# Last weight rows transferred once, rows fetched four slots ahead, routing's product at another slot

## The chip, the cores and the metric

The kernel runs on one core of a Trainium2 chip. The metric is the device time of one execution in microseconds; a lower number is better. The core's engines are TensorE (matmuls; PE in the profile, PEld its weight loads), VectorE (DVE), ScalarE (ACT), GpSimd (POOL) and SyncE (SP), which here only issues transfers. Sixteen DMA engines carry the transfers.

## The reference

Three layers follow one another. The first is a gated linear attention (an mLSTM) over 4 batches, 8 heads, 768 steps, head size 40:

```
m_new = max(f + m, i);  f_s = exp(f + m - m_new);  i_s = exp(i - m_new)
C = f_s * C + i_s * (v k^T);   n = f_s * n + i_s * k
y = sigmoid(o) * (C q) / max(|n q|, 1)
```

The second is a dense layer over 3072 tokens: `h = x @ w_in` (320 to 2048), `x2 = (h * sigmoid(h)) @ w_out` (2048 to 320). The third is a mixture of 8 experts, where each token goes to one expert only:

```
logits = x2 @ w_gate;  e = argmax(logits);  g = softmax(logits)[e]
out = g * (relu(x2 @ w1[e]) @ w2[e])        # w1[e]: 320 x 1024, w2[e]: 1024 x 320
```

Everything is float32.

## The kernel before

Matmuls run in float16 on numbers that are split into a high and a low half; the products of the halves are summed in PSUM. The 320 rows of a weight matrix are two blocks of 128 rows and a last block of 64. For the last 64 rows, the high half lies on partitions 0 to 63 and the low half on partitions 64 to 127 of the same block, so that one matmul takes both.

**The loop.** Steps are cut into 6 chunks of 128 for each of the 4 batches; a chunk and a batch make an attention unit (`n = 4c + b`). The dense layer makes a pass over chunk c with 16 blocks `f` of the inner dimension. Each block has two slots of a plan (`p`), so that a pass has 32 slots. In the even slot TensorE runs `l1` (8 matmuls, L959, tile ps_h), what `run_at(p)` finds planned, and then `l2` of the block two earlier (12 matmuls into ps_y, L1000 to L1005); in the odd slot it runs what is planned there. A function that returns another one has that one run in the next slot (`late`). The order on TensorE, ScalarE, VectorE and SP is that of the program, written out by hand.

The steps of an attention unit are planned at its base `p`: scores S at p and p + 1 (L294, read by VectorE at L296), I at p + 2 (L304, read at L308), C at p + 3 (L353, read at L367), PV at p + 5 (L318, read at L324), X at p + 12 (L394, read by ScalarE at L397 and VectorE at L400). Except for the first units, the bases are 8 slots apart, so that within a chunk's pass S stands at slots 7 and 8, I at 9, C at 10, X of the unit before at 11, PV at 12, S of the next unit at 15. All of them take their PSUM tile from `ps_at`, which has two buffers, in turn. A tile can be written when the readers of the one two tiles earlier are through.

**Routing.** `rows(c)` (L844) is planned into the pass of chunk c + 1 in eight steps, two slots apart, from slot 5 on: `experts`, `scale`, `weights`, `place`, and four `halves`. `place` (L874) runs two small matmuls (L877, L878; the routing's product) into a ps_at tile and four VectorE operations that give each token the number of its row in the tensor rows_x. `halves` splits a batch's 128 results and scatters them to rows_x (L929). For the last chunk these steps are called by hand in the next stage.

**The experts.** The tokens of an expert stand in rows_x in groups of 128 (slots of the list `line`, 28 in all). For three slots (EARLY) the rows are known before the last chunk's routing; `fetch_early` (L1021) loads them, planned at slot 23 of the last pass. For each other slot `fetch` (L1184) reads a row number into a register of SP, loads the 128 rows transposed (L1189) and their scales (L1194). Rows go to buffers in turn (`xT_b`, L1182): four tiles that the attention used (Ks[1], Qs[0], Qs[1], Ks[0]). A slot has two halves of 32 matmuls (`m_half`, L1209) and 24 matmuls of the second layer (`m_l2`, L1228 to L1230). In the loop at L1329, turn i fetches slot i + 3 first.

**The experts' weights.** `load_w` (L532) loads a quarter of an expert: 256 rows of w1, the last 64 rows of w1 (L541, L546), and 256 rows of w2, into a staging buffer. `go` converts it on ScalarE (L552, L553), and `tail` makes the low halves on VectorE (L556, L560, L564). The last 64 rows are loaded twice, to partitions 0 to 63 and 64 to 127, by a source whose outermost dimension has two copies. Sixteen quarters are loaded during the loop and 32 in the expert stage, where `low_and_load`, `split` and `load` keep up to six in flight; one is converted in each turn, two in the odd ones.

Of the kernel before, what the change touches and what calls it, by code (L numbers as in the profile page):

```python
# [8 lines left out]
F32 = mybir.dt.float32  # L9
F16 = mybir.dt.float16  # L10
BF16 = mybir.dt.bfloat16
I32 = mybir.dt.int32
AF = mybir.ActivationFunctionType
# [10 lines left out]
SW1, SW2 = 2.0**10, 2.0**12  # L24
# [3 lines left out]
def bcast0(ap, n):  # L28

    return bass.AP(tensor=ap.tensor, offset=ap.offset, ap=[[0, n]] + list(ap.ap))  # L30
# [3 lines left out]
def mlstm_moe_kernel(ctx, tc, q, k, v, ig, fg, og, w_in, w_out, w_gate, w1, w2, out):  # L34
    nc = tc.nc
# [3 lines left out]
    NC = S // CH  # L39
    DM = H * D  # L40
    FF = w_in.shape[1]
    NF = FF // 128
# [7 lines left out]
    GF = F2 // NG  # L50
# [3 lines left out]
    NE = len(EARLY)  # L54
# [7 lines left out]
    const = ctx.enter_context(tc.tile_pool(name="const", bufs=1))  # L62
# [25 lines left out]
    START, ATTN, FIRST = 0, 2, 4  # L88
# [3 lines left out]
    def carve(where, shape, dtype=F32):  # L92

        n = 1
        for d in shape:
            n *= d
        size = 2 if dtype is F16 else 4
        a = carved[where]
        carved[where] += n * size
        assert carved[where] <= limit[where], (where, carved[where])  # L100
        x = w_all if dtype is F16 else F32V if dtype is F32 else w_all.bitcast(dtype)
        x = x[:, a // size:a // size + n]
        return x if len(shape) == 1 else x.rearrange("p (a b) -> p a b", a=shape[0])

    def turns(views):

        i = 0
        while True:
            yield views[i % len(views)]
            i += 1  # L110
# [7 lines left out]
    for e in range(E):  # L118
# [12 lines left out]
        out=tri, in_=ones, pattern=[[1, 128]], compare_op=ALU.is_gt, fill=0.0, base=0, channel_multiplier=-1  # L131
# [5 lines left out]
    Qs = [const.tile([128, H, 128], F16, name=f"Qs{i}") for i in range(2)]  # L137
    Ks = [const.tile([128, H, 128], F16, name=f"Ks{i}") for i in range(2)]
# [10 lines left out]
    wol = carve(FIRST, (NF, NO), F16)  # L149
    xt_b = turns([carve(FIRST, (6, 512), F16) for _ in range(2)])  # L150
    vw_b, hb_b = carve(FIRST, (H, D1)), carve(FIRST, (H, D1))
    y_b = turns([carve(FIRST, (384,)), const.tile([128, 384], F32, name="y2")])
    cl_b = carve(FIRST, (H, D1), F16)[0:D]
    vh_b, vl_b = [turns([carve(FIRST, (H, D1), F16) for _ in range(3)]) for _ in range(2)]
    late_at = carved[FIRST] // 4
# [376 lines left out]
    def load_w(k, g, e, ts=None):  # L532

        cs = slice(g * GF, (g + 1) * GF)
        if ts is None:
            ts = stg.tile([128, WI], F32, tag="wi", name="e12")
        t = ts[:, 0:3 * GF].rearrange("p (j f) -> p j f", j=3)
        t2 = ts[:, 3 * GF:3 * GF + 2 * DM].rearrange("p (j d) -> p j d", j=2)
        if isinstance(e, int):
            nc.sync.dma_start(out=t[:, 0:2, :], in_=w1[e, 0:256, cs].rearrange("(j p) f -> p j f", p=128))  # L540
            nc.sync.dma_start(out=t[:, 2, :], in_=bcast0(w1[e, 256:320, cs], 2))  # L541
            nc.sync.dma_start(out=t2, in_=w2[e, cs, :].rearrange("(j p) d -> p j d", p=128))
        else:
            ee = bass.ds(e, 1)
            nc.sync.dma_start(out=t[:, 0:2, :], in_=w1[ee, 0:256, cs].rearrange("e (j p) f -> p (e j) f", p=128))
            nc.sync.dma_start(out=t[:, 2, :], in_=w1[ee, 256:320, cs].to_broadcast([2, 64, GF]))  # L546
            nc.sync.dma_start(out=t2, in_=w2[ee, cs, :].rearrange("e (j p) d -> p (e j) d", p=128))
        o1 = w1c[k][:, :, cs]
        o2 = w2c[k][:, 2 * g:2 * g + 2]

        def go():
            nc.scalar.activation(out=o1[:, 0:3, :], in_=t, func=AF.Copy, scale=SW1)  # L552
            nc.scalar.activation(out=o2[:, :, 0, :], in_=t2, func=AF.Copy, scale=SW2)  # L553

            def tail():
                nc.vector.scalar_tensor_tensor(  # L556
                    out=o1[:, 3:5, :], in0=t[:, 0:2, :], scalar=SW1, in1=o1[:, 0:2, :],
                    op0=ALU.mult, op1=ALU.subtract,
                )
                nc.vector.scalar_tensor_tensor(  # L560
                    out=o1[64:128, 2, :], in0=t[64:128, 2, :], scalar=SW1, in1=o1[64:128, 2, :],
                    op0=ALU.mult, op1=ALU.subtract,
                )
                nc.vector.scalar_tensor_tensor(  # L564
                    out=o2[:, :, 1, :], in0=t2, scalar=SW2, in1=o2[:, :, 0, :], op0=ALU.mult, op1=ALU.subtract
                )
            return tail
        return go

    import contextlib  # L570
    with contextlib.nullcontext():

        wg_t = const.tile([128, 3, E], F32, name="wg_t")
        with tc.tile_pool(name="gate", bufs=1) as gp:
# [25 lines left out]
            for i in range(3):  # L600
# [4 lines left out]
                out=mneg, in_=mneg, pattern=[[0, 4], [1, CH]], compare_op=ALU.is_ge, fill=-1e30,  # L605
# [74 lines left out]
            def first(b, g):  # L680
# [95 lines left out]
                out=E_t[:, 1:, :], in0=E_t[:, 1:, :], scalar1=1.0 / (SQ * SQ), scalar2=None, op0=ALU.mult  # L776
# [12 lines left out]
        def at(p, fn, *args):  # L789
            plan.setdefault(p, []).append((fn, args))  # L790
# [6 lines left out]
        for n in range(B, NC * B):  # L797
            cb = divmod(n, B)
            p = base[n]
# [23 lines left out]
        for f in range(NF):  # L823
# [7 lines left out]
            p = 2 * f - 2  # L831
# [4 lines left out]
        for i in range(4 * NG):  # L836
            p = 2 * NF * 2 + 10 * i if i < 2 * NG else 2 * NF * (NC - 1) - 7 + 7 * (i - 2 * NG) // 2
# [100 lines left out]
            return [experts, scale, weights, place] + [lambda b=b: halves(b) for b in range(nb)]  # L938

        for c in range(NC - 1):  # L940
            for i, fn in enumerate(rows(c)):
                at(2 * NF * (c + 1) + 5 + 2 * i, fn)
        at(2 * NF * (NC - 1) + 23, lambda: fetch_early())

        gt = {}
        l2b = {}
# [74 lines left out]
        def fetch_early():  # L1021
            for i, (e, n) in enumerate(EARLY):
                o = e * ER + 128 * (n + 1)
                r = rows_x[o:o + 128, :]
                xT[e, n] = (Qs + Ks)[i][:, 0:6, :]
                nc.sync.dma_start_transpose(out=xT[e, n], in_=r.bitcast(F16)[:, 0:768])
                xm[e, n] = xms[:, i, :]
                nc.sync.dma_start(out=xm[e, n], in_=r[:, 384:386])
            pe = ps_at.tile([128, E], F32, tag="at", name="ps_e")
            nc.tensor.matmul(pe, ones, cum[:, NTT - B, :], start=True, stop=True)  # L1030
            nc.vector.memset(done, 0.0)
            for e, n in EARLY:
                nc.vector.tensor_scalar(
                    out=done[:, e:e + 1], in0=pe[:, e:e + 1], scalar1=128.0 * (n + 1), scalar2=None, op0=ALU.min
                )
# [22 lines left out]
        p = 0  # L1058
# [3 lines left out]
        for c, b0, b1 in passes:  # L1062
# [17 lines left out]
            if c == 0:  # L1080
                for r in rowt:
# [4 lines left out]
                    out=rows_x.rearrange("(e r) w -> r e w", e=E)[0:128],  # L1086
                    in_=rowt[0].unsqueeze(1).to_broadcast([128, E, RW]),
# [4 lines left out]
        while plan or late:  # L1092
            p = min([*plan, *late])
# [85 lines left out]


        hT, place_of = {}, {}
        xT_b = turns([x[:, 0:6, :] for x in Ks[1:] + Qs + Ks[:1]])  # L1182

        def fetch(i, row):  # L1184

# [96 lines left out]
        def low_and_load():  # L1282

            if w_low:
                t, place = w_low.pop(0)
                t()
                load(place)

        def get(i):
            if NE <= i < len(line):  # L1290
                fetch(line[i][0], line[i][2])

        def second(i):
            m_l2(line[i][0], line[i][1], line[i][3])
# [3 lines left out]
        with tc.manual_schedule(engines=by_hand):  # L1298

            for cf in todo:  # L1300
                l2(*cf)
            for i in range(2):
                rowt.append(th_v[i][:, 0:RW])
                nc.gpsimd.memset(rowt[-1][:, 352:384], 0.0)
            experts, scale, weights, place, *halves = rows(NC - 1)
            half = lambda i, r: m_half(line[i][0], line[i][1], r)
            t = half(0, 0)
            experts()
            t()
            t = half(0, 1)  # L1310
            place()
            scale()
            weights()
            t()
            h = [x() for x in halves[0:2]]
            t = half(1, 0)
            h.pop(0)()
            t()
            h += [x() for x in halves[2:]]
            h.pop(0)()  # L1320
            t = half(1, 1)
            h.pop(0)()
            h.pop(0)()
            count()
            t()
            second(0)
            get(NE)
            get(NE + 1)
            for i in range(2, len(line)):  # L1329
                get(i + 3)  # L1330
                t = half(i, 0)
                low_and_load()
                t()
                if i > 5 and i % 2:
                    split()
                t = half(i, 1)
                t()
                if i > 5 and i % 2:
                    low_and_load()
                if i == 3:  # L1340
                    later_slots()
                split()
                if more and i > 4:
                    load(more.pop(0))
                second(i - 1)
            second(len(line) - 1)
        n_slots = nc.values_load(eni[0:1, E - 1:E], min_val=0, max_val=128 * NSLOT)
        with tc.If(n_slots > 128 * ND):
            for i in range(ND, NSLOT):
                name, k, row, no = later(i)  # L1350
                e = nc.sync.value_load(evi[0:1, i:i + 1], min_val=0, max_val=E - 1)
# [36 lines left out]
```

## Time and profile before

| | us |
|---|---|
| median of 3 runs | 732.72 (732.57 to 733.4) |
| the profiled execution | 736.41 |
| its span, first to last instruction | 734.7 |
| TensorE busy in the span | 671.2 (91%) |
| VectorE busy | 529.7 (72%) |
| ScalarE busy | 372.7 (51%) |
| DMA queue of SP and ScalarE (q1), share of 16 engines | 63.8% |

Times of rows count from the start of the span. Busy time says how long an engine worked; an engine's idle time matters only where the next work on the path waits. The clock of a stretch (PEclk) is the granted share of TensorE's full 2.4 GHz, so 0.5 is 1.2 GHz. The DMA share is the mean over sixteen engines; a transfer's whole time counts in the stretch in which its packets start, so a short stretch can have more than 1.

### The profile page before, as it was taken

The page shows a single profiled execution, that of the slowest core. Times are in us where ns is not written, and L with a number is a line of the kernel's source. Part 1 is how long each engine was busy: PE and PEld are TensorE (multiplying, and loading weights), DVE is VectorE, ACT ScalarE, POOL GpSimd, SP SyncE. Part 2 cuts the span into 40 slices and gives each one's busy share as a digit, 9 for nine tenths or more (in the row PEclk, how much of TensorE's full clock was granted, in tenths as well). Part 3 has the DMA queues.
Part 4 walks back from the last instruction along what each step waited for, and adds up shares of the span by engine and source line. Part 5 has one row for each costly group of instructions (what it writes and reads, how often), then busy time and mean ns, then how long its engine had stood idle before and what let it go on. Part 6 is the DMA issues. An engine that isn't in the chain of part 4 may idle for free.

```text
span 734.7 us, 15579 instructions
## 1 busy us (share of the span) xinstructions
PE 671.2 (91%) x5840; PEld 480.0 (65%) x5840; DVE 529.7 (72%) x1262; ACT 372.7 (51%) x816; POOL 100.6 (14%) x134
## 2 busy tenths in 40 slices
PE   3868899999899989998999999999999898998993
PEld 2734666776476655665666665556888786877882
DVE  7775779987888787799887975975677655665631
ACT  4644365655575655675676635564334333533410
POOL 3100011100121002110210110020311111111111
PEclk9758599999999988999999999999999999999998
DMA  8768979884565655976587520544279799999900
GB/s 158 128 150 205 201 144 212 196 198 88 106 139 127 138 100 106 166 149 131 116 180 162 133 80 14 128 146 105 80 145 194 166 189 171 186 170 190 160 24 15
DMA packets 242828, 102.82 MB, mean 140 GB/s; under 512 B 181141, under 2 KB 236632, under 8 KB 242744
## 3 DMA queue, kind: packets, MB, share of 16 engines
q1 hardware_dynamic: 239380, 92.98, 63.8%
q0 software_dynamic: 2880, 8.68, 3.5%
q8 instruction: 48, 0.79, 0.5%
q14 instruction: 36, 0.29, 0.2%
q10 hardware_dynamic: 484, 0.08, 0.1%
HBM read 71.64 MB, written 11.59 MB: 113 GB/s over the span
## 4 chain that ended last, share of the span: by engine, by line
PE 70%; DVE 13%; DMA 8%; ACT 3%; SPq 3%; issue 2%; POOL 0%; POOLq 0%; DVEq 0%; ACTq 0%
PE ps_h L959 19%; PE ps_m L1209 12%; PE ps_y L1003 5%; PE ps_y L1005 5%; PE ps_y L1004 5%; PE ps_pv L318 5%; DMA Ks<-rows_x 3%; PE ps_y L1000 3%; PE ps_m L1228 3%; PE ps_m L1230 3%; PE ps_m L1229 3%; DMA Qs<-rows_x 2%; PE ps_wg L517 1%; DMA wi<-in_moe_w_in_dram 1%; DMA w_all<-lam_d 1%
## 5 line engine op out<-in xcount | busy, mean ns | idle before, releaser
L959 PE MATMUL ps_h<-w_all 128*128 128x512 f16 x768 | 193.1, 392 | 8.2 <-ACT w_all L466 5.1
L959 PEld LDWEIGHTS <-w_all 128*128 128x128 f16 x768 | 73.5, 100 | 85.1 <-issue 10.6
L1209 PEld LDWEIGHTS <-w_all 128*128 128x128 f16 x1792 | 106.8, 101 | 19.1 <-DMA Ks<-rows_x 9.9
L1005 PE MATMUL ps_y<-w_all 128*128 128x328 f16 x332 | 101.1, 305 | 0.3 <-DVE w_all L986 0.3
L1004 PE MATMUL ps_y<-w_all 128*128 128x328 f16 x332 | 101.1, 305 | 0.0
L1003 PE MATMUL ps_y<-w_all 128*128 128x328 f16 x332 | 100.9, 305 | 0.0
L1214 ACT ACTIVATE hh<-ps_m 128x512 f16<-128x512 f32 x56 | 33.3, 596 | 126.5 <-PE ps_m L1209 114.9
L975 ACT ACTIVATE w_all<-ps_h 128x512 f32<-128x512 f32 x83 | 49.2, 592 | 67.0 <-PE ps_h L959 66.8
L978 DVE SCALAR_TENSOR_TENSOR w_all<-w_all,ps_h 128x512 f32<-128x512 f32 x83 | 56.7, 683 | 29.3 <-ACT w_all L975 28.0
L1215 DVE SCALAR_TENSOR_TENSOR hl<-ps_m,hh 128x512 f16<-128x512 f32 x56 | 38.6, 690 | 48.5 <-ACT hh L1214 48.1
L983 ACT ACTIVATE w_all<-w_all 128x512 f16<-128x512 f32 x83 | 51.6, 622 | 30.7 <-DVE w_all L978 28.9
L1229 PE MATMUL ps_m<-w_all,hh 128*128 128x320 f16 x224 | 67.0, 299 | 0.0
L1230 PE MATMUL ps_m<-w_all,hl 128*128 128x320 f16 x224 | 67.0, 299 | 0.0
L1228 PE MATMUL ps_m<-w_all,hh 128*128 128x320 f16 x224 | 67.0, 299 | 0.0
L1209 PE MATMUL ps_m<-Ks,w_all 128*128 128x128 f16 x896 | 55.9, 226 | 8.9 <-DMA Ks<-rows_x 6.9
L986 DVE SCALAR_TENSOR_TENSOR w_all<-w_all 128x512 f16<-128x512 f32 x83 | 57.9, 697 | 5.6 <-ACT w_all L983 5.3
L1209 PE MATMUL ps_m<-Qs,w_all 128*128 128x128 f16 x896 | 54.1, 222 | 6.0 <-DMA Qs<-rows_x 4.2
L1240 POOL DMA_INDIRECT out_dram<-ym,sid x28 | 32.0, 1142 | 169.5 <-DVE sid L1239 153.7
L318 PEld LDWEIGHTS ps_pv<-w_all 128*128 128x128 f32 x384 | 51.2, 210 | 4.3 <-issue 1.7
L318 PE MATMUL ps_pv<-w_all 128*128 128x41 f32 x384 | 51.2, 296 | 0.4 <-DVE w_all L296 0.4
L241 ACT ACTIVATE w_all<-w_all,bias_t 128x128 f32<-128x128 f32 x160 | 50.2, 391 | 2.4 <-POOL w_all L207 2.3
L207 POOL TENSOR_SCALAR_AFFINE_SELECT w_all<-w_all 128x1024 f32<-128x1024 f32 x20 | 22.8, 1142 | 183.1 <-DMA w_all<-lam_d 130.0
(219 smaller groups left out, 1159.6 us busy)
## 6 DMA issues: line engine op xcount, KB each, us to landing
e<-in_moe_w_dram SPq DMA_DIRECT2D x35, 320.0 KB
w_all<-lam_d SPq DMA_DIRECT2D x20, 512.0 KB
e<-in_moe_w_dram SPq DMA_DIRECT2D x35, 256.0 KB
w_all<-in_moe_w_out_dram SPq DMA_DIRECT2D x16, 320.0 KB
e<-in_moe_w_dram SPq DMA_DIRECT2D x35, 128.0 KB
w_all<-in_moe_w_dram SPq DMA_DIRECT2D x13, 320.0 KB
wi<-in_moe_w_in_dram SPq DMA_DIRECT2D x8, 512.0 KB
w_all<-in_k_dram SPq DMA_DIRECT2D x24, 160.0 KB
```

The lines of the kernel that those rows point to most:

```text
L318: nc.tensor.matmul(pv[:, h, :], u["lam"][:, h, :], u["v"][:, h, :], start=True, stop=True)
L959: nc.tensor.matmul(ps, a, x, start=(i == 0), stop=(i == len(terms) - 1))
L978: nc.vector.scalar_tensor_tensor(out=th, in0=th, scalar=1.0, in1=ps, op0=ALU.add, op1=ALU.mult)
L983: nc.scalar.activation(out=gh, in_=th, func=AF.Copy, scale=SG)
L986: nc.vector.scalar_tensor_tensor(out=gl, in0=th, scalar=SG, in1=gh, op0=ALU.mult, op1=ALU.subtract)
L1003: nc.tensor.matmul(ps, gh[:, ts], woh[:, f, :], start=(f == 0), stop=False)
L1004: nc.tensor.matmul(ps, gh[:, ts], wol[:, f, :], start=False, stop=False)
L1005: nc.tensor.matmul(ps, gl[:, ts], woh[:, f, :], start=False, stop=(f == NF - 1))
L1209: nc.tensor.matmul(ps[:, jj, :], w1c[k][:, a, f * 128:f * 128 + 128], x[:, m, :], start=(n == 0), stop=(n == len(terms) - 1),)
L1228: nc.tensor.matmul(ps, hh[:, f, :], w[:, 0, :], start=(f == 0), stop=False)
L1229: nc.tensor.matmul(ps, hh[:, f, :], w[:, 1, :], start=False, stop=False)
L1230: nc.tensor.matmul(ps, hl[:, f, :], w[:, 0, :], start=False, stop=(f == NF2 - 1))
```

## The change

Three edits. First, the last 64 rows of w1 are loaded once, to partitions 0 to 63. ScalarE's conversion becomes two instructions, of 128x512 and of 64x256, and VectorE makes the low half by reading partitions 0 to 63 and writing 64 to 127. Second, a fifth buffer for fetched rows, the tile y2, which the attention used before, and fetches four slots ahead instead of three: three fetches stand before the loop instead of two. Third, the eight steps of `rows(c)` stand at slots 5, 7, 9, 13, 14, 16, 18, 20 instead of 5, 7, 9, 11, 13, 15, 17, 19, and `fetch_early` at 24 instead of 23.

```
-    y_b = turns([carve(FIRST, (384,)), const.tile([128, 384], F32, name="y2")])
+    y2 = const.tile([128, 384], F32, name="y2")
+    y_b = turns([carve(FIRST, (384,)), y2])
...
-            nc.sync.dma_start(out=t[:, 2, :], in_=bcast0(w1[e, 256:320, cs], 2))
+            nc.sync.dma_start(out=t[0:64, 2, :], in_=w1[e, 256:320, cs])
...
-            nc.sync.dma_start(out=t[:, 2, :], in_=w1[ee, 256:320, cs].to_broadcast([2, 64, GF]))
+            nc.sync.dma_start(out=t[0:64, 2, :], in_=w1[ee, 256:320, cs].rearrange("e p f -> p (e f)"))
...
-            nc.scalar.activation(out=o1[:, 0:3, :], in_=t, func=AF.Copy, scale=SW1)
+            nc.scalar.activation(out=o1[:, 0:2, :], in_=t[:, 0:2, :], func=AF.Copy, scale=SW1)
+            nc.scalar.activation(out=o1[0:64, 2, :], in_=t[0:64, 2, :], func=AF.Copy, scale=SW1)
...
-                    out=o1[64:128, 2, :], in0=t[64:128, 2, :], scalar=SW1, in1=o1[64:128, 2, :],
+                    out=o1[64:128, 2, :], in0=t[0:64, 2, :], scalar=SW1, in1=o1[0:64, 2, :],
...
-            for i, fn in enumerate(rows(c)):
-                at(2 * NF * (c + 1) + 5 + 2 * i, fn)
-        at(2 * NF * (NC - 1) + 23, lambda: fetch_early())
+            for i, fn in zip((5, 7, 9, 13, 14, 16, 18, 20), rows(c)):
+                at(2 * NF * (c + 1) + i, fn)
+        at(2 * NF * (NC - 1) + 24, lambda: fetch_early())
...
-        xT_b = turns([x[:, 0:6, :] for x in Ks[1:] + Qs + Ks[:1]])
+        xT_b = turns(
+            [Ks[1][:, 0:6, :], y2.bitcast(F16).rearrange("p (j t) -> p j t", j=6)]
+            + [x[:, 0:6, :] for x in Qs + Ks[:1]]
+        )
...
             get(NE + 1)
+            get(NE + 2)
             for i in range(2, len(line)):
-                get(i + 3)
+                get(i + 4)
```

## Rows read from the trace of the kernel before

**Rows 1.** The page: the chain that ended last, and a group of TensorE's matmuls.
```profile
PE 70%; DVE 13%; DMA 8%; ACT 3%; SPq 3%; issue 2%; POOL 0%; POOLq 0%; DVEq 0%; ACTq 0%
...
L959 PE MATMUL ps_h<-w_all 128*128 128x512 f16 x768 | 193.1, 392 | 8.2 <-ACT w_all L466 5.1
```

**Rows 2.** Waits of TensorE: who for whom, us in total, times, longest.
```profile
PE ps_m L1209 <- DMA Ks<-rows_x: 6.9, 3, 3.5
...
PE ps_r L877 <- DVE w_all L367: 2.9, 2, 1.5
...
PE ps_r L877 <- DVE w_all L296: 2.7, 1, 2.7
```

**Rows 3.** Windows, expert stage: us, busy us of PE PEld DVE ACT POOL, PEclk, DMA, GB/s.
```profile
509.40:723.20 213.80, 198.40 (x2468) 170.29 (x2466) 126.55 (x280) 78.83 (x127) 35.11 (x31) 0.98 0.79 145
...
512.00:518.00 6.00, 4.05 (x69) 3.68 (x67) 5.34 (x28) 3.01 (x7) 0.00 (x0) 1.00 0.00 0
...
542.00:544.00 2.00, 1.61 (x14) 1.06 (x12) 1.97 (x4) 0.25 (x1) 0.80 (x1) 1.00 0.74 147
...
584.00:592.00 8.00, 5.37 (x56) 4.85 (x55) 2.52 (x6) 0.68 (x2) 1.18 (x1) 0.79 0.84 150
618.00:626.00 8.00, 4.49 (x51) 4.42 (x51) 2.85 (x6) 1.00 (x2) 1.18 (x1) 0.79 1.11 190
666.00:674.00 8.00, 4.92 (x57) 4.62 (x55) 3.02 (x6) 1.19 (x2) 1.18 (x1) 0.79 0.85 148
```

**Rows 4.** Windows, for the last two columns (DMA share, GB/s).
```profile
552.00:554.00 2.00, 2.00 (x40) 2.00 (x38) 1.59 (x4) 0.60 (x1) 1.01 (x1) 1.00 1.04 314
...
597.20:678.40 81.20, 71.79 (x875) 61.65 (x873) 47.02 (x84) 31.97 (x50) 11.77 (x10) 0.96 1.04 178
632.00:634.00 2.00, 2.00 (x36) 1.92 (x33) 1.48 (x2) 0.77 (x2) 0.33 (x1) 1.00 0.14 48
...
695.00:700.00 5.00, 5.00 (x59) 4.09 (x57) 1.99 (x6) 1.97 (x4) 0.00 (x0) 1.00 0.62 130
```

**Rows 5.** Timeline of TensorE: first-layer matmuls of two slots (start, us, what).
```profile
550.74 3.74 PE L1209 MATMUL ps_m<-Ks,w_all 128*128 128x128 f16 x64
...
557.57 3.74 PE L1209 MATMUL ps_m<-Ks,w_all 128*128 128x128 f16 x64
```

**Rows 6.** Timeline of SP: issues of fetches and loads (start, us, what).
```profile
493.89 1.24 SPq L1026 DMA_TRANSPOSE Qs<-rows_x  x1
...
597.21 1.53 SPq L1189 DMA_TRANSPOSE Qs<-rows_x  x1
...
669.51 1.27 SPq L1189 DMA_TRANSPOSE Ks<-rows_x  x1
...
672.26 0.38 SPq L545 DMA_DIRECT2D e<-in_moe_w_dram  x1
...
674.66 0.37 SPq L545 DMA_DIRECT2D w_all<-in_moe_w_dram  x1
...
678.36 2.49 SPq L1189 DMA_TRANSPOSE Ks<-rows_x  x1
```

**Rows 7.** Around the routing's product: three windows, one row of VectorE's timeline.
```profile
192.00:200.00 8.00, 5.17 (x48) 2.41 (x47) 5.91 (x15) 1.23 (x2) 0.00 (x0) 0.79 0.81 143
...
270.00:281.00 11.00, 11.00 (x42) 6.88 (x41) 6.29 (x18) 4.52 (x13) 2.25 (x3) 0.53 0.62 142
...
344.00:348.00 4.00, 2.57 (x19) 1.54 (x17) 3.60 (x11) 1.43 (x4) 0.00 (x0) 1.00 1.03 184
...
347.32 0.54 DVE L400 SCALAR_TENSOR_TENSOR w_all<-ps_x,w_all 128x384 f16<-128x384 f32 x1
```

**Rows 8.** Groups by shape on ScalarE: count | busy us, mean ns.
```profile
L552 ACT ACTIVATE w_all<-e 128x768 f16<-128x768 f32 x35 | 29.2, 835 | 0.7 <-DMA e<-in_moe_w_dram 0.7
...
L466 ACT ACTIVATE w_all<-w_all 64x128 f16<-64x128 f32 x24 | 7.3, 304 | 0.3
...
L466 ACT ACTIVATE w_all<-w_all 128x512 f16<-128x512 f32 x8 | 5.0, 623 | 5.0 <-DVE w_all L428 5.0
```

## The prediction

> **What bounds the kernel now.** I read the page first, then the waits of TensorE, then windows over the last stage, then the DMA shares there, and last the places where the routing's product stands. The page's chain is 70% TensorE and 8% DMA [rows 1]: the kernel is bound by TensorE, so what can be won is the time in which TensorE stands still or runs at its lower clock. The waits show two causes that the change touches: the expert matmuls (L1209) wait for the transposed rows, and the routing's product (L877) waits for VectorE's reads of ps_at buffers, 2.7 us once and 2.9 us in two further rounds [rows 2]. In the expert stage, 213.8 us long, TensorE is busy 198.40 us [rows 3]. Of the 15.4 us idle, 1.95 lie at its start around the last routing (512 to 518) and 0.39 at 542 to 544; the other 13.1 are stalls ahead of a slot's first matmul. After the three longest the granted clock falls from 2.4 to 1.2 GHz for a while: 0.79 on the mean of each of three stretches of 8 us [rows 3], (1 - 0.79) x 8 = 1.7 us each, 5.0 in all. A little of that low clock lies in the idle time itself, so both together make 17.5 us.
>
> Why are the rows late? From 597.2 to 678.4 the DMA share is 1.04 [rows 4], so the fetch waits in a full queue. But the bytes don't explain it: 178 GB/s there against 314 GB/s at share 1.04 between 552 and 554. In between stand stretches like 632 to 634, where the share is 0.14 and the rate 48 GB/s [rows 4]: two engines of sixteen (0.125) still work on something and the rest stand. That fits L541 and L546, whose outermost dimension is two copies: 64 rows of 1 KB on each of two engines. A transposed fetch has its part on every engine, so I read it as landing only when these two are through.
>
> The count confirms it. Two slots bring three loads and two fetches. L541's 131 KB at 48 GB/s are 2.7 us on the two engines; the other 590 KB of a load at 314 GB/s are 1.9 us on every engine; a fetch takes about 1.1 us (695 to 700, mostly three fetches, 0.62 x 5 = 3.1 us) [rows 4]. Sum on the two engines: 3 x 4.6 + 2 x 1.1 = 16.0 us. SP's fetches of every second slot stand at 597.21 and, five pairs later, at 678.36: 16.2 us a pair [rows 6]. TensorE needs 6.83 us a slot without a stall [rows 5], 13.7 a pair. The two engines are 2.5 us a pair too slow, and SP, blocked behind them, falls back until every second slot stalls.
>
> **The change part by part.** *The last 64 rows once.* The transfer halves to 65 KB and its outermost dimension becomes 64 rows. No row shows a 64-row transfer from memory in this queue. If it spreads like the 128-row ones, it is 65 KB at 314 GB/s, 0.2 us; at worst, all on one engine at half of 48 GB/s, it is 2.7 us again. I take 0.2: rows of whole partitions are what the 128-row transfers have, and those run at the full rate. Then a pair costs 3 x (1.9 + 0.2) + 2 x 1.1 = 8.5 us on each engine, well under 13.7, and the stalls have no cause. What is late next is SP's own issuing: a fetch takes it 2.75 us (669.51 to 672.26), a load 2.40 (672.26 to 674.66) [rows 6], 2 x 2.75 + 3 x 2.40 = 12.7 a pair, still under 13.7. So all 17.5 us go.
>
> The Trainium skill, DMA: Bandwidth & Descriptors, section Rules for kernel authors, says that a leading broadcast of c copies confines a transfer to c engines and that an outermost size that is a multiple of 16 uses all; by it the new transfer is 0.2 us, and an estimate by it gives the same 17.5. The same section speaks against the change where it advises 128 partitions and 1 MiB a transfer, and calls transfers under 64 KB mostly overhead; the new one sits on that border. The trace has 14 engines of 16 standing during the old transfer [rows 4], so an overhead would have room, and it would change no term.
>
> *ScalarE and VectorE.* The conversion of 128x768 (0.835 us) becomes 128x512 and 64x256 [rows 8]. 128x512 is 0.623; 64x256 lies between 0.304 (64x128) and 0.623, by elements about 0.41. That is 0.2 us more for each of 48 conversions, 9.5 us of ScalarE (bounds 0.09 and 0.41, 4.4 and 19.7 us). ScalarE is on 3% of the chain [rows 1]; in the expert stage it is busy 78.83 of 213.8 us [rows 3], and its idle time hides it. In the loop, where conversions precede VectorE's work ahead of a wait, a few can show: 0.6 us. If ScalarE had no idle time, all 9.5 would count. VectorE's third operation keeps its size and reads other partitions: 0, with nothing in the rows for a gain or a loss.
>
> *Four ahead in five buffers.* The buffer of slot i+4 is that of slot i-1, as the buffer of i+3 was, so no new wait for a buffer. One fetch more is issued ahead of the first load, 2.75 us of SP, while the loads are needed many slots later. It gives one slot, 6.83 us, of further lead. With the queue relieved it hides nothing that is left: 0. If the queue were not relieved it would be worth up to 6.8 us once.
>
> *The product between two units.* At slot 11 it takes the next ps_at buffer right behind C and X, and waits until VectorE has read C (L367) or, in the first round, the second scores (L296) [rows 2]. At slot 13 it stands behind PV and twelve ps_y matmuls and takes the buffer of X, which VectorE reads at 347.32 for 0.54 us (third round) [rows 7], some 3 us earlier. Behind it on TensorE stand the next ps_h matmuls, which no longer wait. First round: of 2.7 us part returns, since C now needs the buffer that the product waited for; eight ps_h matmuls lie between, 193.1 / 96 = 2.0 us [rows 1], so 0.7 returns and 2.0 go; the low clock around it, 0.79 over 8 us [rows 7], partly idle, gives 1.3: 3.3. Second round: 1.5 of wait, and the low clock that follows, (1 - 0.53) x 11 = 5.2 [rows 7]: 6.7. X's own shorter wait there stays, but the third round had 1.4 of wait at clock 1.00 [rows 7], so a wait of that size need not lower the clock. Third round: 1.4. Fourth and fifth: 0. Sum 11.4. Bounds: 0 if VectorE's backlog stops the next TensorE instruction instead, 12.1 if nothing returns. The row scatters move one slot later and the early fetch too, some 1.7 us; it is issued at 493.89 and used from 509.4 [rows 6, 3], so that costs 0.
>
> **Sum.** -17.5 - 11.4 + 0.6 = -28.3. The profiled execution took 736.41 us (span 734.7 and 1.7 around it): 708.1. The median of the runs is 732.72, 3.7 us less than the profiled one, so some term is smaller in them. If none of these, 704.4; if the long low-clock stretch (5.2) is what they lack, 709.6. I take 706, its own range 700 to 712.
>
> **The rivals.** *VectorE takes the product's place.* In the third round VectorE is busy 3.60 of 4 us [rows 7]; whatever TensorE wins it may wait for at the next read. Then only the expert stage gains: 732.7 - 17.5 = 715.2. Against it: between these spots TensorE is the one that is full.
>
> *The fetches stay late.* The 64 rows don't spread, or SP paces. Then the product's 11.4 and one slot's lead, 6.8, remain: 732.7 - 11.4 + 0.6 - 6.8 = 715.1, or 721.9 if the lead is eaten too. For it: SP's 12.7 is not far below 13.7. Against: SP's spacing of 16.2 is the two engines' sum.
>
> *Slower: the product stalls at its new place.* At slot 13 VectorE has the seven operations of PV's end in its queue, and the product's buffer could come free behind them. If each of four rounds then waits 2.7 us and loses 5.2 to the clock, that is 31.6 against 12.1 now, +19.5, against -17.5: 734.7. It decides from about 4.4 us of further cost a round. Against it: the read that frees the buffer stands ahead of PV's end in VectorE's order.
>
> **How the numbers follow.** Forecast 0.82; VectorE 0.06; late fetches 0.06; slower 0.04; no difference by both halves eaten 0.02. The range 700 to 717 takes in the first two rivals' 715 and leaves out the rest. Faster by over 0.2% (1.5 us, about what can be told from no change) 0.94, within it 0.02, slower 0.04.
>
> **What would show it.** Right: no stretch with a share of 0.14 at 48 GB/s in the expert stage, no L1209 wait on rows_x beyond a microsecond, expert slots 6.83 us apart, the stage about 196 us, no L877 wait between 190 and 350, clock 1.00 at the place of 270 to 281. Wrong: fetches still 16 us a pair; new waits of S or C on VectorE of the size of those gone; a low clock elsewhere.

## The result

The changed kernel takes 707.62 us (median of 4 runs, 699.15 to 714.71) beside 732.64 us of the kernel before: a ratio of 0.962, with a 95% interval of 0.9536 to 0.9704. The forecast was 706. Ratios and their intervals go by the fast runs of a kernel alone, medians by all of its runs, so that where many runs are slow the two can differ. The profiled execution took 707.71 us, 28.7 us less than that of before (736.41); the sum of the prediction was 28.3. The near agreement of these two is partly luck, as the experiments show.

The page of the changed kernel: the chain, the waits of TensorE in the expert stage (from 500 us on), and windows of the loop and of the stage (columns as in [rows 3]).

```profile
PE 79%; DVE 12%; ACT 3%; DMA 2%; issue 2%; SPq 1%; POOL 0%; POOLq 0%; DVEq 0%; ACTq 0%
```

```profile
PE ps_m L1214 <- DVE hl L1220: 1.4, 2, 0.8
PE ps_r L879 <- DVE cum L872: 0.5, 1, 0.5
PE ps_m L1214 <- DMA e<-in_moe_w_dram: 0.4, 1, 0.4
```

```profile
163.20:499.60 336.40, 331.41 (x2494) 212.22 (x2492) 279.22 (x683) 206.62 (x459) 46.54 (x46) 1.00 0.55 124
499.60:694.20 194.60, 192.24 (x2469) 165.89 (x2466) 124.58 (x280) 81.29 (x159) 35.11 (x31) 1.00 0.62 149
...
270.00:281.00 11.00, 11.00 (x95) 6.60 (x93) 10.07 (x30) 7.86 (x19) 2.91 (x3) 1.00 0.48 110
584.00:592.00 8.00, 8.00 (x111) 7.05 (x109) 4.51 (x9) 3.81 (x8) 1.18 (x1) 1.00 0.80 204
```

DMA fell from 8% to 2% of the chain [rows 1]. In the kernel before, fetches stood on the chain for 6.3 to 8.8 us from issue to landing (start, us; two of five), and TensorE waited for rows_x by the line in [rows 2] and by the last of these:

```profile
597.21 6.98 DMA Qs<-rows_x
...
612.70 8.84 DMA Ks<-rows_x
```

```profile
PE ps_m L1209 <- DMA Qs<-rows_x: 4.2, 2, 3.1
```

In the changed kernel no fetch stands on the chain of the expert stage, and no wait for rows_x is left. The expert stage, 213.8 us at clock 0.98 [rows 3], takes 194.6 at 1.00, and its idle time falls from 15.4 to 2.4 us. The DMA share there falls from 0.79 to 0.62 while the rate stays (145 and 149 GB/s): the same flow keeps the engines busy for less of the time. The loop from the second dense pass on takes 336.4 us; the same stretch of the kernel before is this row:

```profile
161.30:509.40 348.10, 338.49 (x2495) 215.32 (x2494) 278.82 (x683) 205.22 (x443) 43.90 (x46) 0.98 0.56 124
```

Three cuts from the timelines of the changed kernel (start, us). The first shows SP's fetches for every second slot, the second the first-layer matmuls of two slots in a row, the third C and the product in the first round of the loop:

```profile
583.21 1.26 SPq L1194 DMA_TRANSPOSE Qs<-rows_x  x1
...
596.76 1.27 SPq L1194 DMA_TRANSPOSE Ks<-rows_x  x1
...
610.45 1.27 SPq L1194 DMA_TRANSPOSE Qs<-rows_x  x1
```

```profile
547.25 3.74 PE L1214 MATMUL ps_m<-Ks,w_all 128*128 128x128 f16 x64
554.08 3.74 PE L1214 MATMUL ps_m<-Ks,w_all 128*128 128x128 f16 x64
```

```profile
197.22 0.18 PE L354 MATMUL ps_c<-w_all,Ks 128*40 128x41 f16 x1 [0.92 <-DVE w_all L297]
...
199.59 0.18 PE L879 MATMUL ps_r<-cum,ones 128*128 128x32 f16 x1
```

Every second fetch is now 13.6 us after the last one instead of 16.2 [rows 6]: that is two of TensorE's slots (6.83 us, as in [rows 5]), so TensorE sets the pace and no longer waits for the fetches. In the loop the product no longer waits (the 0.5 us in the waits above belong to the one after the loop, as before); C takes over 0.92 us of the 2.7, as the prediction had it (0.7).

### The profile page after: what moved, and what is told of

Same layout as the page of the kernel before. It is cut to its first block, busy times and chain, and to the rows that moved or that the text cites. A ratio compares the mean times of both kernels' runs of the same rounds, so it can differ in the third digit from the quotient of the medians.

```text
span 705.6 us, 15619 instructions
## 1 busy us (share of the span) xinstructions
PE 662.0 (94%) x5840; PEld 475.6 (67%) x5840; DVE 526.7 (75%) x1262; ACT 376.4 (53%) x864; POOL 102.9 (15%) x134
## 4 chain that ended last, share of the span: by engine, by line
PE 79%; DVE 12%; ACT 3%; DMA 2%; issue 2%; SPq 1%; POOL 0%; POOLq 0%; DVEq 0%; ACTq 0%
PE ps_h L961 20%; PE ps_m L1214 13%; PE ps_pv L319 6%; PE ps_y L1005 5%; PE ps_y L1007 5%; PE ps_y L1006 5%; PE ps_m L1233 4%; PE ps_m L1235 4%; PE ps_m L1234 4%; PE ps_y L1002 4%; PE ps_s L295 1%; PE ps_wg L518 1%; PE ps_x L395 1%; DMA wi<-in_moe_w_in_dram 1%; PE ps_c L354 1%
## 5 line engine op out<-in xcount | busy, mean ns | idle before, releaser
L961 PE MATMUL ps_h<-w_all 128*128 128x512 f16 x768 | 190.3, 388 | 6.1 <-ACT w_all L467 3.3
L961 PEld LDWEIGHTS <-w_all 128*128 128x128 f16 x768 | 73.0, 100 | 81.1 <-issue 8.5
L1214 PEld LDWEIGHTS <-w_all 128*128 128x128 f16 x1792 | 102.4, 98 | 4.3 <-issue 1.3
L319 PEld LDWEIGHTS ps_pv<-w_all 128*128 128x128 f32 x384 | 52.7, 215 | 4.2 <-issue 1.7
L208 POOL TENSOR_SCALAR_AFFINE_SELECT w_all<-w_all 128x1024 f32<-128x1024 f32 x20 | 22.1, 1107 | 176.7 <-DMA w_all<-lam_d 104.4
L1214 PE MATMUL ps_m<-Qs,w_all 128*128 128x128 f16 x768 | 45.0, 219 | 1.8 <-DVE hl L1220 1.4
L931 POOL DMA_INDIRECT rows_x<-w_all,di x24 | 27.8, 1157 | 114.4 <-DVE w_all L988 54.2
```

Source lines behind the costliest of these rows:

```text
L319: nc.tensor.matmul(pv[:, h, :], u["lam"][:, h, :], u["v"][:, h, :], start=True, stop=True)
L961: nc.tensor.matmul(ps, a, x, start=(i == 0), stop=(i == len(terms) - 1))
L1214: nc.tensor.matmul(ps[:, jj, :], w1c[k][:, a, f * 128:f * 128 + 128], x[:, m, :], start=(n == 0), stop=(n == len(terms) - 1),)
```

## The experiments

Theory: a transfer with two copies outermost runs on two of the sixteen engines, and these two pace the expert stage; the product's place is worth what it waits; the longer lead hides nothing once the queue is relieved. Rivals: the lead is what removes the stalls; or the halved bytes are. Times are medians of 6 to 12 runs, where nothing else is said, in three series, each beside the kernel before (729.81, 729.99 and 731.05 us). Gains in us "by the ratio" are what the ratio takes off these medians.

**The whole change again** (no edit).

> The changed kernel once more, unaltered, as the measure for the others and to see how far its runs lie apart. All theories: about 707.6 us, within the 699 to 715 that its first four runs spanned. If the spread belongs to the kernel, it shows again; if it came from the chip of that day, the runs lie within about 1 us.

706.57 us (702.25 to 710.25), ratio 0.9686 (0.9648 to 0.9724). The spread shows again, and in both kernels: the 18 runs of before in this series lie between 725.79 and 733.12. Where it arises is told at the end.

**Each part alone.**

```
-            nc.sync.dma_start(out=t[:, 2, :], in_=bcast0(w1[e, 256:320, cs], 2))
+            nc.sync.dma_start(out=t[0:64, 2, :], in_=w1[e, 256:320, cs])
...
```

> The last 64 rows once, alone; fetches three ahead and the product at slot 11 as before. Theory (the two-copy transfer holds two DMA engines, and they pace the expert stage): the stalls ahead of expert slots and their low clock go, -17.5, ScalarE's second instruction +0.6: about 715.5 us, expert stage about 196 us. Rival (the lead of four slots is what removes the stalls, the transfer only saves 65 of 721 KB): a pair of slots falls from 16.2 to about 15.2 us, still over 13.7, less than half of the stalls go: about 724.

710.94 us, ratio 0.9745 (0.971 to 0.9781): 18.9 us less by the median, 18.6 by the ratio. Its loop and stage:

```profile
156.70:499.20 342.50, 333.19 (x2494) 212.77 (x2493) 279.03 (x683) 207.09 (x459) 43.65 (x46) 1.00 0.54 122
499.20:694.30 195.10, 192.48 (x2469) 165.94 (x2466) 125.40 (x281) 81.36 (x159) 35.11 (x31) 1.00 0.67 149
```

With fetches only three slots ahead the stage takes 195.1 us, the same as in the whole change: the rival of the lead falls.

```
-                at(2 * NF * (c + 1) + 5 + 2 * i, fn)
+            for i, fn in zip((5, 7, 9, 13, 14, 16, 18, 20), rows(c)):
+                at(2 * NF * (c + 1) + i, fn)
...
```

> The product at slot 13 (and the four row steps and the early fetch behind it) alone. Theory (TensorE's wait for the ps_at buffer, and the low clock that follows in two rounds): -11.4, about 721 us, no wait of the product in the loop, clock 1.00 where it was low after 270. Rival (VectorE's backlog stops the next TensorE instruction instead): about 732.

725.23 us, ratio 0.9916 (0.9877 to 0.9956): 4.6 us less by the median, 6.1 by the ratio (3.2 to 9.0). The expectation of 11.4 less was too much; the loop, alone in the first row, takes 336.3 us as in the whole change, and the stage in the second keeps its stalls:

```profile
165.50:501.80 336.30, 331.56 (x2495) 212.00 (x2493) 278.48 (x683) 204.92 (x443) 47.47 (x46) 1.00 0.59 128
501.80:715.20 213.40, 198.23 (x2468) 170.09 (x2466) 126.72 (x280) 78.77 (x127) 35.11 (x31) 0.98 0.81 145
```

```
-        xT_b = turns([x[:, 0:6, :] for x in Ks[1:] + Qs + Ks[:1]])
+        xT_b = turns(
+            [Ks[1][:, 0:6, :], y2.bitcast(F16).rearrange("p (j t) -> p j t", j=6)]
+            + [x[:, 0:6, :] for x in Qs + Ks[:1]]
+        )
...
+            get(NE + 2)
             for i in range(2, len(line)):
-                get(i + 3)
+                get(i + 4)
```

> Four slots ahead in five buffers alone. Theory: the two DMA engines still need 16.2 us a pair against 13.7; the longer lead is used up once, between 0 and -6.8: 726 to 732 us, stalls begin a turn or two later. Rival (the lead removes the stalls): -17, about 715.

727.78 us, ratio 0.9901 (0.9864 to 0.9937): 2.0 us less by the median, 7.2 by the ratio (4.6 to 9.9). The 12 runs lie between 717.72 and 737.52, so the times alone don't size it. Its stage, one of its waits, and two of SP's fetches, five pairs of slots apart, show where the lead went:

```profile
501.10:712.90 211.80, 196.65 (x2469) 168.78 (x2466) 125.73 (x280) 81.32 (x127) 33.03 (x31) 0.98 0.84 146
```

```profile
PE ps_m L1213 <- DMA Ks<-rows_x: 4.9, 2, 4.4
```

```profile
590.51 2.75 SPq L1193 DMA_TRANSPOSE y<-rows_x  x1
...
670.80 2.00 SPq L1193 DMA_TRANSPOSE y<-rows_x  x1
```

The stalls on rows_x remain (idle 15.1 us, clock 0.98), and the pairs are 16.1 us apart, as before (16.2). The stage is 1.0 to 2.0 us shorter than in the two profiles of before (213.8, and 212.8 in the second one, shown further down): the lead is used up once and the two engines pace as before. By the medians the three parts give 18.9 + 4.6 + 2.0 = 25.5 us against 23.2 of the whole in the same series; by the ratios 18.6 + 6.1 + 7.2 = 31.9 against 22.9. The times thus don't show that the parts add up.

**Bytes or engines.** The first of these two keeps both copies, and so the bytes, but spreads them; the second has the rows once, and so half of the bytes, but 61 of the 64 rows in one transfer.

```
-            nc.sync.dma_start(out=t[:, 2, :], in_=bcast0(w1[e, 256:320, cs], 2))
+            for h0 in (0, 64):
+                nc.sync.dma_start(out=t[h0:h0 + 64, 2, :], in_=w1[e, 256:320, cs])
```

> The kernel before, with the doubled 64 rows fetched as two transfers of 64 rows each instead of one with two copies: the same 131 KB as before, the same conversion, one transfer more for SP to issue in each load, but each spread by rows. Theory (what matters is that two engines carry it all): a load is 1.9 + 0.4 us on every engine, the stalls go, expert stage 195 to 200 us (SP needs up to 0.6 us more a load, 14.5 us a pair against 13.7, so a stall or two may stay), about 712 to 718 us beside 730 of before. Rival (it is the bytes, or the halved transfer): nothing changes, stage 213, about 730.

```
-            nc.sync.dma_start(out=t[0:64, 2, :], in_=w1[e, 256:320, cs])
+            nc.sync.dma_start(out=t[0:61, 2, :], in_=w1[e, 256:317, cs])
+            nc.sync.dma_start(out=t[61:64, 2, :], in_=w1[e, 317:320, cs])
```

> The last 64 rows once, as in e2_rows_once, but as two transfers of 61 and 3 rows: half of the bytes, the new conversion, and as many transfers as in e6_two_transfers. The Trainium skill, DMA: Bandwidth & Descriptors, section Why a DMA increments its semaphore by 16 and not by 1, says that the number of engines divides the outermost size, so that 61 rows go to one engine. Theory: 62 KB on one engine at half of 48 GB/s are 2.6 us, as long as the old transfer held its two, so a pair needs about 16 us again and the stalls return: stage 210 to 218, 725 to 732 us. Rival (half of the bytes is what helped): stage about 196, 711 us as e2_rows_once.

The first takes 712.25 us, ratio 0.9734 (0.9684 to 0.9784). Its profile is that of its longest run, 720.24 us, whose loop starts as late as 169.2 us; its stage is the row that follows:

```profile
511.60:706.20 194.60, 192.23 (x2469) 165.82 (x2466) 125.28 (x280) 78.44 (x127) 35.05 (x31) 1.00 0.66 159
```

The second takes 721.08 us, ratio 0.9883 (0.983 to 0.9935). Its stage, a stretch within it, and most of its waits for rows_x:

```profile
500.40:706.90 206.50, 194.76 (x2469) 166.90 (x2466) 125.10 (x280) 81.30 (x159) 35.03 (x31) 0.99 0.76 141
```

```profile
558.00:560.00 2.00, 2.00 (x23) 1.58 (x21) 0.89 (x2) 1.37 (x4) 0.00 (x0) 1.00 0.07 23
```

```profile
PE ps_m L1212 <- DMA Ks<-rows_x: 5.4, 4, 1.8
```

Two of its fetches, six pairs of slots apart (start, us):

```profile
569.45 1.83 SPq L1192 DMA_TRANSPOSE Ks<-rows_x  x1
...
662.80 1.67 SPq L1192 DMA_TRANSPOSE Ks<-rows_x  x1
```

All the bytes of before, spread, give the whole gain of the stage (194.6 us), with the conversions of before. Half of the bytes, most of them on one engine, bring the waits for rows_x back, with as many transfers for SP to issue as in the first. And the stretch of share 0.07 at 23 GB/s, one engine of sixteen (0.0625), has taken the place of 0.14 at 48 [rows 4]. So it is the number of engines, not the bytes. The Trainium skill's rule (DMA: Bandwidth & Descriptors, section Why a DMA increments its semaphore by 16 and not by 1), by which the number of engines divides the outermost size, told the one engine in advance, and the trace agrees, with the share of 0.07. The size was off: 206.5 us, where 210 to 218 were expected. The one engine exceeds TensorE's 13.7 us a pair by less, its fetches being 15.6 us a pair apart.

**The lead, with the queue relieved** (the whole change with `get(i + 3)` and four buffers).

> The whole change without the fourth slot of lead and the fifth buffer. Theory (with the queue relieved the lead hides nothing): the same as the whole change, 706.6 us within 1.5, expert stage 195. Rival (the lead adds its part to the others): 2 us slower, as four ahead alone was 2.0 us faster than before.

701.38 us, ratio 0.9646 (0.9589 to 0.9703), 5 us below the whole change of the series before. That fits neither theory, so both ran side by side once more:

> The whole change without the fourth slot of lead and the fifth buffer once more, beside the whole change. It took 701.4 us where the whole change had taken 706.6 in another call; both spread over 10 us. Theory (the lead does nothing once the queue is relieved, and the 5 us are the spread of the first 160 us): medians within 3 us of each other, intervals that overlap, expert stages of 195 us in both. Rival (the fourth slot of lead costs 5 us): 5 us apart again, with the same sign.

> The changed kernel once more, in the same call as the two others, as their measure: 706 us, runs between 699 and 712.

706.01 us without the lead (698.18 to 707.92) and 703.58 with it (699.31 to 713.98); ratios 0.9688 (0.9634 to 0.9742) and 0.9637 (0.9577 to 0.9698); stages of 195.3 and 195.4 us. The sign turned: with the queue relieved, the lead does nothing that can be told from the spread.

**The low clock of the second round** (the kernel before, unaltered).

> The kernel before once more, for one question: is the low clock between 270 and 281 there again? The forecast counted its 5.2 us as something the product's new place wins. If it belongs to the wait at slot 11, the second round of the loop loses 5 us again. If it is chance, as e2_rows_once and e4_ahead suggest, which have the same waits without it, the loop's second round is at clock 1.00.

One run, 733.86 us. The product in the second round; the loop, the expert stage, and the window behind that product:

```profile
273.29 0.18 PE L877 MATMUL ps_r<-cum,ones 128*128 128x32 f16 x1 [1.46 <-DVE w_all L367]
```

```profile
165.40:508.10 342.70, 333.34 (x2495) 212.79 (x2493) 278.62 (x683) 205.17 (x443) 44.55 (x46) 1.00 0.56 126
508.10:720.90 212.80, 198.10 (x2468) 170.25 (x2466) 125.80 (x280) 78.92 (x127) 35.09 (x31) 0.98 0.80 145
...
274.00:285.00 11.00, 11.00 (x78) 7.32 (x77) 9.19 (x25) 7.17 (x18) 3.23 (x3) 1.00 0.61 144
```

The same wait of 1.46 us, and the clock stays at 1.00. Six profiles have the product at slot 11 (the two of before, rows once alone, four ahead alone, two transfers, 61 and 3 rows). One alone has the low clock there, and its loop takes 348.1 us; four others take 342.4 to 342.9. The sixth, 61 and 3 rows, takes less:

```profile
159.80:500.40 340.60, 331.76 (x2494) 212.33 (x2492) 278.41 (x683) 206.65 (x459) 45.25 (x46) 1.00 0.55 123
```

It differs in the first round. There the clock falls behind the product's longer wait (2.65 us) in five of the six profiles, and not in this one. The 4 us behind the product, in the second profile of before and in that of 61 and 3 rows:

```profile
199.55:203.55 4.00, 4.00 (x36) 2.00 (x36) 2.68 (x8) 0.60 (x1) 0.00 (x0) 0.62 1.05 187
```

```profile
193.95:197.95 4.00, 4.00 (x45) 2.41 (x45) 3.23 (x9) 0.81 (x2) 0.00 (x0) 1.00 1.15 192
```

So the same wait can be followed by the low clock or not: by some 2.65 us in five of six, by 1.46 us in one of six. What decides it in an execution is not shown.

**The same form elsewhere.** The last 64 rows of w_in come by a two-copy transfer too.

```
-            out=t[:, 2 * n:], in_=bass.AP(tensor=r.tensor, offset=r.offset, ap=[[n // 2, 2]] + list(r.ap))
+        r2 = win_v[256:320, f2 * n + n // 2:(f2 + 1) * n]
+        nc.sync.dma_start(out=t[0:64, 2 * n:], in_=r)
+        nc.sync.dma_start(out=t[64:128, 2 * n:], in_=r2)
...
```

> The whole change, and the other transfer of the two-copy form spread as well: the last 64 rows of w_in (131 KB, eight times in the first 160 us) as two transfers of 64 rows. Theory (a transfer whose outermost size is two holds two engines for 2.7 us and whatever needs all engines waits): in the profile of e7_rows_once_place one load of w_in takes 6.3 us to land on the chain and the first passes wait 5.4 us for its conversion; the landing falls to 3 to 4 us, 2 to 4 us of the whole go: 703 us beside the whole change at 706. Rival (in the first 160 us the conversion on VectorE and ScalarE is what paces, and the low clock there): no difference within 2 us.

695.42 us (691.74 to 699.92), ratio 0.9559 (0.95 to 0.9617), 8.2 us below the whole change beside it, the shortest median of all. It beats the kernel before by 32.2 us by the ratio (28.0 to 36.6), the whole change beside it by 26.5 (22.1 to 30.9); since these intervals overlap, the step between the two is likely but not sure. One load on the chain of waits (start, us) of this kernel, and then of the whole change beside it:

```profile
65.19 3.79 DMA wi<-in_moe_w_in_dram
```

```profile
63.80 6.60 DMA wi<-in_moe_w_in_dram
```

The landing of this load takes 2.8 us less, as expected. The median gained more, and that is not settled: the stretch up to the second pass took 149.6 us here and 160.0 there, but 152.8 in the profile without the lead, which has the two-copy transfer.

## Why the prediction was right, and where it was not

**The two engines.** Right, and shown from both sides: bytes kept and spread, bytes halved and confined. The term was 17.5 us; the stage fell by 19.2 in the profiles (213.8 to 194.6), and the part alone measured 18.9 by the median (16.0 to 21.2 by the ratio). Of the 19.2, 13.0 were idle time, as the prediction had it (13.1), and 6.2 busy time, where it had counted the low clock of three stretches alone, 5.0 at most.

**The 64-row transfer.** It spreads, as the value taken at 0.2 us supposed, though its own time was not read: of the windows of 1 us from 540 to 650, thirteen of the kernel before have a share of 0.12 to 0.15 at 43 to 54 GB/s, and none of the changed kernel has.

**SP's issuing.** It stays under TensorE's pace: fetches 13.6 us a pair apart, which is TensorE's own 13.7.

**Four ahead.** 0 on top, as forecast; alone 1.0 to 2.0 us of the stage, of the 6.8 that bounded it.

**ScalarE.** The two instructions of a conversion, count | busy us, mean ns:

```profile
L553 ACT ACTIVATE w_all<-e 128x512 f16<-128x512 f32 x35 | 21.7, 621 | 0.0
L554 ACT ACTIVATE w_all<-e 64x256 f16<-64x256 f32 x35 | 14.1, 404 | 0.0
```

Together they take 0.19 us more than the one instruction (0.2 forecast). A part on the path was not seen: the loop of rows once alone (342.5 us) equals that of before without the low clock (342.7). The 0.6 were none.

**The product's place.** The waits went as forecast, 0.92 coming back at C. But the term of 11.4 us was mis-sized. The second round's "1.5 of wait, and the low clock that follows, (1 - 0.53) x 11 = 5.2" took for a consequence of the wait what one profile in six shows. Without the 5.2 the term is 6.2. The loop of before is 342.7 us without that low clock, so the place is worth 342.7 - 336.3 = 6.4 us in the profiles, and 4.6 by the median, 6.1 by the ratio (3.2 to 9.0), in the times. The first round's 1.3 for the clock holds in five profiles of six; in the sixth the loop is 340.6 us, and the place would be worth 4.3. The prediction itself had the sign of it: a wait of the same size in the third round left the clock at 1.00, and the timed runs were 3.7 us faster than the profiled one.

**The total.** That 28.3 met 28.7 is luck of the profile of before, which has the low clock: its loop is 348.1 us and that of the changed kernel 336.4, 11.7 less, of which 5.4 are that event (348.1 - 342.7). With the 19.2 of the stage this makes 30.9; the stretch before the loop, which the change was not to touch, came out 1.9 us longer (161.3 and 163.2), so that the spans differ by 29.1. The medians fell by 25.0 us (732.64 to 707.62), near 19.2 + 6.4. The forecast of 706 met them because it stood between 704.4, the sum taken whole, and 709.6, the sum without the 5.2, while the stage gave 1.7 us more than its term. Of the rivals, none took place.

## What to carry to other kernels

Look at short windows of the DMA share and the rate together. In this kernel a share of 0.14 at 48 GB/s, while fetches wait, was a transfer on two engines of sixteen, and 0.07 at 23 GB/s one on a single engine; the same 131 KB a load made a stage of 213.8 us on two engines and one of 194.6 us spread. The cure was an outermost dimension of 64 rows, with all of the bytes or with half of them; 61 rows outermost were no cure. Other transfers of the same form are worth a trial. A low clock that one profile shows after a wait should not be counted in full until a second profile shows it again.

## What was not expected

Runs of one kernel lie up to 20 us apart (717.72 to 737.52 with four ahead alone). Where this arises can be seen in the profiled runs alone. In two profiles of the whole change (707.71 and 703.36 us) loop and expert stage agree to within a microsecond (336.4 and 194.6; 335.6 and 195.4), and 3.2 of the 4.4 us between them lie before the second dense pass. That point was reached at 161.3 and 165.4 us in the two profiles of before, and between 149.6 and 169.2 in the profiles of all versions; the granted clock of that stretch differs too, for example in the profile without the lead and in that of the whole change beside it:

```profile
0.00:152.80 152.80, 127.71 (x881) 88.98 (x882) 121.24 (x299) 88.13 (x248) 19.83 (x57) 0.90 0.87 188
```

```profile
0.00:160.00 160.00, 132.30 (x881) 92.72 (x882) 123.36 (x299) 88.50 (x248) 20.12 (x57) 0.86 0.84 179
```

What sets it in an execution was not tried.
